# Half of d_ff as seven block products for eight, and w_in kept in DRAM: a packed-attention and FFN kernel on one core

## The chip, the cores and the metric

The kernel runs on one core of one Trainium2 chip. The metric is the device time of one execution in microseconds; several runs of one kernel are summed up by their median. The engines are named as the profile names them: PE (TensorE, matrix products; PEld are its weight loads), DVE (VectorE), ACT (ScalarE), POOL (GpSimd), SP (SyncE, which issues nearly all DMAs). Each takes its instructions from a queue of its own, in order, and waits on semaphores for the others.

## The reference

Two small attentions, one behind the other, feed a feed-forward product. There are 8 batches, 8 heads, 576 rows of 64 columns, and 32 packed rows p for each head. All data is float32.

```python
p_packed = sm_attn(p, k, v)             # softmax(p k^T / 8) v : 32 rows a head
attn_out = sm_attn(q, p_packed, p_packed)
x = attn_out.transpose(0, 2, 1, 3).reshape(B * S, H * D)   # 4608 x 512
h = x @ w_in                            # 512 x 2048
g = h * np.clip(h + 3.0, 0.0, 6.0) / 6.0
out = g @ w_out                         # 2048 x 512
```

## The kernel before

**Numbers.** Each float32 operand of the two large products is split into a high part that TensorE takes in one pass and a low part, the rest; a product is three matmuls: high by high, high by low, low by high. For x @ w_in the kernel does not form x: it multiplies w_in by the packed rows first (m, 256 by 2048 for a batch, `u_m`, matmuls at L339, split at L525 and L527), and the first product is then m by the attention weights a.

**Tiles.** d_ff is cut into 16 tiles f of 128, d_model stays whole, 512 columns, one PSUM bank. The 576 rows of a batch go through in two chunks, c = 0 and c = 1; one is narrow (256 rows) and one wide (320 rows: 256 and an edge of 64). The edges of an even batch and the odd one after it are joined to one block of 128 rows, which the wide chunk of the odd batch multiplies. In even batches the wide chunk is c = 1, in odd ones c = 0. A step s = 16c + f of batch b does:
- `first_product`: six matmuls (L921) into one of two PSUM tiles `ps_hh`, 256 or 320 columns each;
- `gated`: relu on ACT (L933), min and multiply on DVE (L934), the cast to the high part on ACT (L940), the low part on POOL (L941); edges alike (L946, L947);
- `second_product` (L952): three matmuls of 512 columns for each 128 rows, into accumulators that stay open over the 16 steps. Its call is put into `pend` and made two steps later, so that two first products lie between a gate and its use.

At f = 15 the accumulators are scaled on ACT (L911) and stored (L912).

**Order.** Batch 0 follows a list written by hand (`PLAN`). For batches 1 to 7 the Tile scheduler orders the instructions; `fill(c, f)` gives it, ahead of each step, pieces of the next batch's work: three chains (`inputs`: loads and transposes of k and q; `packed`: the first attention and its product with v; `ahead`: the second attention's weights `u_s2`), begun at the steps that `STAGES` names, so many pieces a step. From step `SOON` = 24 the first two quarters of the next batch's m are made, `u_m(b+1, 0, 1)`, as one block of 32 small matmuls on TensorE; the last two are made at the start of that batch, `u_m(b, 2, 3)`, spread by `LATE`. w_in stays in SBUF throughout as four tiles of 1 MB, one for each quarter of d_ff (`w_in0` to `w_in3`). The packed attention's product with v (L458) reads `v_nat` and `v_high`, loaded on SP.

## Time and profile before

| | |
|---|---|
| median of 3 runs | 720.01 us (719.67 to 720.78) |
| profiled execution | span 718.5 us; its own time is among those of the runs, which lie 1.2 to 2.3 us above the span |
| mean granted TensorE clock in it | 0.990 |
| PE busy | 699.5 us, 97% |
| ACT, DVE, POOL busy | 387.9, 345.9, 255.2 us |
| DMA | 55.97 MB, mean 78 GB/s |

One execution is profiled; its span is counted from the first to the last instruction on the core. In rows that name a line, an engine, an operation and tiles (out<-in), the numbers behind the bar are busy time and the mean duration of one in ns, then the idle time of the engine ahead of them and what ended it. In timeline rows the first number is the start in us from the begin of the span, the second the duration; "x2" stands for two instructions in one row.

### The profile page before, as it was taken

How to read it: one execution, taken by the hardware profiler on the slowest of the kernel's cores; microseconds unless marked ns; L12 is line 12 of the kernel's file. 1: busy time of each engine (PE TensorE's matmuls, PEld its weight loads, DVE VectorE, ACT ScalarE, POOL GpSimd, SP SyncE). 2: the span in 40 equal slices, each digit the busy share in tenths (PEclk: the TensorE clock that was granted, in tenths of full speed). 3: DMA queues.
4: the chain of work that ended last, by engine and by line, in shares of the span. 5: the costliest groups of instructions: out<-in, count | busy, mean ns of one | idle time of the engine just before them, and what ended most of it. 6: DMA issues, size and time to landing. Idle time of an engine off the chain costs nothing.

```text
span 718.5 us, 13932 instructions
## 1 busy us (share of the span) xinstructions
PE 699.5 (97%) x5168; PEld 572.7 (80%) x5168; DVE 345.9 (48%) x725; ACT 387.9 (54%) x916; POOL 255.2 (36%) x391
## 2 busy tenths in 40 slices
PE   6599999999999999999999999999999999999998
PEld 4477877788788878888788888888878887888886
DVE  2887788341844274441555338433184426431111
ACT  5799976444555356543555446544455535553343
POOL 1565641232223344323322234332322324433332
PEclk9699999999999999999999999999999999999999
DMA  9989853335015510433104440133401510000010
GB/s 287 307 210 232 226 138 94 49 63 119 1 26 100 103 35 1 96 63 75 45 1 96 75 92 1 34 67 71 106 2 28 93 39 31 1 31 0 1 45 30
DMA packets 191029, 55.97 MB, mean 78 GB/s; under 512 B 172528, under 2 KB 184304, under 8 KB 190960
## 3 DMA queue, kind: packets, MB, share of 16 engines
q1 hardware_dynamic: 190416, 54.88, 32.7%
q8 instruction: 40, 0.66, 0.4%
q10 hardware_dynamic: 544, 0.20, 0.1%
q14 instruction: 29, 0.24, 0.1%
HBM read 45.61 MB, written 9.44 MB: 77 GB/s over the span
## 4 chain that ended last, share of the span: by engine, by line
PE 89%; DVE 3%; DMA 2%; ACT 2%; SPq 2%; issue 1%; POOL 0%; DVEq 0%; ACTq 0%
PE acc L952 53%; PE ps_hh L921 23%; PE ps_h L595 3%; PE ps L339 3%; PE ps_x L339 2%; SPq L284 1%; PE ps L458 1%; DMA nat<-in_q_dram 1%; DMA v_high<-in_v_dram 1%; PE ps_t L666 1%; DVE tr L543 1%; PE ps L428 1%; DMA k_nat<-in_k_dram 1%; PE ps L263 1%; PE ps_w L708 0%
## 5 line engine op out<-in xcount | busy, mean ns | idle before, releaser
L952 PE MATMUL acc<-wo_hi,g 128*128 128x512 f32 x896 | 319.0, 397 | 0.0
L941 POOL TENSOR_TENSOR g<-t,g 128x256 fp32r<-128x256 f32 x224 | 166.3, 743 | 408.1 <-ACT g L940 396.4
L934 DVE SCALAR_TENSOR_TENSOR t<-t,ps_hh 128x320 f32<-128x320 f32 (+1 forms) x224 | 100.9, 450 | 243.6 <-ACT t L933 242.7
L952 PEld LDWEIGHTS acc<-wo_hi,g 128*128 128x128 f32 x896 | 168.3, 188 | 42.8 <-issue 5.3
L933 ACT ACTIVATE t<-ps_hh,three 128x320 f32<-128x320 f32 (+1 forms) x224 | 111.9, 500 | 165.7 <-PE ps_hh L921 160.9
L952 PE MATMUL acc<-wo_lo,g 128*128 128x512 f32 x448 | 176.9, 395 | 0.0
L940 ACT CAST g<-t 128x256 fp32r<-128x256 f32 x224 | 90.8, 405 | 93.7 <-DVE t L934 92.2
L921 PE MATMUL ps_hh<-a_hi,m_hi 128*128 128x320 f32 (+1 forms) x448 | 133.9, 299 | 0.0
L921 PE MATMUL ps_hh<-a_hi,m_lo 128*128 128x320 f32 (+1 forms) x448 | 132.7, 296 | 0.0
L921 PE MATMUL ps_hh<-a_lo,m_hi 128*128 128x320 f32 (+1 forms) x448 | 132.7, 296 | 0.0
L921 PEld LDWEIGHTS ps_hh<-a_hi,m_hi 128*128 128x128 f32 x448 | 84.4, 188 | 11.9 <-issue 1.4
L952 PEld LDWEIGHTS acc<-wo_lo,g 128*128 128x128 f32 x448 | 84.7, 189 | 11.1 <-issue 0.8
L921 PEld LDWEIGHTS ps_hh<-a_lo,m_hi 128*128 128x128 f32 x448 | 84.6, 189 | 8.5
L921 PEld LDWEIGHTS ps_hh<-a_hi,m_lo 128*128 128x128 f32 x448 | 84.7, 189 | 0.9 <-issue 0.9
L543 DVE STREAM_TRANSPOSE tr<-nat 128x576 f32<-128x576 f32 x56 | 42.7, 768 | 36.8 <-DMA nat<-in_k_dram 19.2
L947 POOL TENSOR_TENSOR bnd_lo<-t,bnd_hi 128x64 fp32r<-128x64 f32 x112 | 39.4, 352 | 0.0
L946 ACT CAST bnd_hi<-t 128x64 fp32r<-128x64 f32 x112 | 27.0, 241 | 0.0
L952 PE MATMUL acc<-wo_hi,gh 128*128 128x512 f32 x64 | 26.2, 410 | 0.0
L952 PE MATMUL acc<-wo_lo,bnd_hi 128*128 128x512 f32 x64 | 25.3, 395 | 0.0
L952 PE MATMUL acc<-wo_hi,bnd_hi 128*128 128x512 f32 x64 | 25.1, 393 | 0.0
L952 PE MATMUL acc<-wo_hi,gl 128*128 128x512 f32 x64 | 25.1, 393 | 0.0
L952 PE MATMUL acc<-wo_hi,bnd_lo 128*128 128x512 f32 x64 | 25.1, 392 | 0.0
(181 smaller groups left out, 838.0 us busy)
## 6 DMA issues: line engine op xcount, KB each, us to landing
out_dram<-osb SPq DMA_DIRECT2D x36, 256.0 KB, 2.2
nat<-in_k_dram SPq DMA_DIRECT2D x112, 72.0 KB, 2.6
nat<-in_q_dram SPq DMA_DIRECT2D x112, 72.0 KB, 2.5
raw_out<-in_moe_w_out_dram SPq DMA_DIRECT2D x10, 512.0 KB, 5.1
raw_in<-in_moe_w_in_dram SPq DMA_DIRECT2D x10, 512.0 KB, 5.3
v_nat<-in_v_dram SPq DMA_DIRECT2D x28, 128.0 KB, 2.7
v_high<-in_v_dram SPq DMA_DIRECT2D x56, 64.0 KB, 2.2
raw<-in_moe_w_out_dram SPq DMA_DIRECT2D x4, 512.0 KB, 6.9
```

Of the source, the lines that this page charges most:

```text
L263: nc.tensor.matmul(banks[x][NPK * a:NPK * a + NPK, :n * P], state["pp"][half, NPAIR * x + a], cols[half, :, a], start=True, stop=True,)
L339: nc.tensor.matmul(pair[x][NPK * a:NPK * a + NPK, :n], rows[half, a], c, start=True, stop=True)
L543: nc.vector.transpose(out=t, in_=state.pop(("nat", which, b, a)))
L595: nc.tensor.matmul(h[:, hf, :HS], mm[:, g, fs], aa[:, hf * HS:(hf + 1) * HS], start=(g == 0 and i == 0), stop=(g == NG - 1 and i == 2),)
L921: state["first"] = nc.tensor.matmul(h[:, :n], mm[:, g, fs], aa[:, t0:t0 + n], start=(g == 0 and i == 0), stop=(g == NG - 1 and i == 2),)
L933: state["relu"] = nc.scalar.activation(out=t[:, :n], in_=h, func=AF.Relu, bias=three)
L934: state["gate"] = nc.vector.scalar_tensor_tensor(out=t[:, :n], in0=t[:, :n], scalar=6.0, in1=h, op0=ALU.min, op1=ALU.mult)
L940: nc.scalar.copy(out=gh, in_=tm)
L941: nc.gpsimd.tensor_sub(out=gl, in0=tm, in1=gh.bitcast(F32))
L946: nc.scalar.copy(out=bh, in_=tb)
L947: nc.gpsimd.tensor_sub(out=bnd_lo[:, slot:slot + REM], in0=tb, in1=bh.bitcast(F32))
L952: nc.tensor.matmul(acc, gg, wo_at(part, f), start=(f == 0 and i == 0), stop=(f == NF - 1 and i == 2),)
```

## The change

**Pairs.** From batch 2 on, tiles f = 0 to 7 are taken as four pairs. For a pair (f, f+1) and 256 rows the second product is a 2x2 by 2x2 block product (row blocks of 128 by the two tiles; the two tiles by the two 256-column halves of w_out). It is done with Strassen's scheme in Winograd's form: seven block products instead of eight, each of three matmuls of 256 columns, on sums of blocks. Tiles 8 to 15 stay as they were ("singles").

- Sums of the gated tiles: four DVE instructions of 128 columns for a pair, behind the odd step's gate; then splits on ACT and POOL of 256, 512 and 128 columns (`split`).
- Sums of w_out: `T1`, `T2`, `T4` with their splits go into the buffers of w_in1 to w_in3, T3 over a half of w_out itself. They are made once, in the second chunk of batch 1 (`combine`, a third of a pair's yields a step from f = 4 on).
- Four accumulators A to D (`roles`): A and B take their block products and all singles; C and D are summed at the last pair (one ACT copy, one POOL add, three DVE instructions) and added to A and B at the end by DVE, where ACT copied before.
- The product of the joined edges takes a pair's tiles with the sums that are there, nine matmuls (three of 512 columns, six of 256) instead of six of 512. Edges are kept as float32 (`bnd`) and split late (`edge_parts`).

**w_in.** Since its buffers are taken, w_in is written to DRAM in batch 1 (`keep_w_in`, four DMAs of 1 MB), and for each later batch fetched back one quarter at a time into the one buffer left (`fetch_w_in`). `v_nat` takes turns in that buffer. So m is made in blocks of one quarter: 0, 1, 2 from step 21 on, quarter 3 in the first steps of the next batch. `u_s2` takes one half of the rows at a time in batches 3 to 7, and `STAGES` for the later batches lets the packed attention start at step 10 and takes one piece of the last chain a step.

```diff
-STAGES = ((0, 1), (6, 2), (19, 2))
-
-
-SOON = 24
-LATE = ((3, 2, 1, 2, 1), (3, 1, 1, 1, 0))
+STAGES = (((0, 1), (6, 2), (19, 2)), ((0, 1), (10, 2), (19, 1)))
+
+
+LATE = (3, 2, 1, 2, 1)
+PAIRS = 4
...
-        t = state["v", b] = ap.tile([P, NPAIR, NST, D], F32, name="v_nat", tag="v_nat", bufs=1)
+        home, tag = (wr, "w_in0") if steady else (wp, "v_nat")
+        t = state["v", b] = home.tile([P, NPAIR, NST, D], F32, name="v_nat", tag=tag, bufs=1)
...
+    def edge_product(acc, f, hi, lo, summed, first, last):
+
...
+        i = f // 2
+        second_product(f, acc, *lhs(0), first=first, last=False)
+        product(acc[:, :H2], lhs(1), block(i, "B21"))
+        product(acc[:, H2:], lhs(2), block(i, "B22"))
...
+    def combine(i):
+
...
+        x = [xp.tile([P, 6 * P], F32, name="wx", tag="raw") for _ in range(2)]
+        for k in range(2):
+            hi, lo = (wo_at(part, 2 * i + k).bitcast(F32) for part in ("hi", "lo"))
+            nc.gpsimd.tensor_tensor(out=x[k][:, :DM], in0=hi, in1=lo, op=ALU.add)
+            yield
+        b11, b12, t1 = (x[0][:, k * H2:(k + 1) * H2] for k in range(3))
+        b21, b22, t2 = (x[1][:, k * H2:(k + 1) * H2] for k in range(3))
+        nc.vector.tensor_sub(out=t1, in0=b12, in1=b11)
+        nc.vector.tensor_sub(out=t2, in0=b22, in1=t1)
+        yield
+        nc.vector.tensor_sub(out=b12, in0=b12, in1=b22)
+        nc.vector.tensor_sub(out=b21, in0=b21, in1=t2)
+        yield
+        for name, made in (("T1", t1), ("T2", t2), ("T4", b21), ("T3", b12)):
+            hi, lo = block(i, name)
+            nc.scalar.copy(out=hi, in_=made)
+            nc.vector.tensor_sub(out=lo, in0=made, in1=hi.bitcast(F32))
+            yield
+
+    def moe_pairs(b, c, fill):
+
+        even = b % 2 == 0
+        wide = (c == 1) == even
...
+        def pair_product(i, hi0, lo0, hi1, lo1):
+            at = {"A11": 0, "S1": 1, "S2": 2, "S3": 3, "A12": 4, "A22": 5, "S4": 6}
+
+            def lhs(name):
+                k = at[name]
+                return [(z[k // 4])[:, (k % 4) * P:(k % 4 + 1) * P] for z in ((hi0, hi1), (lo0, lo1))]
+
+            order = [
+                ("A", 0, "A12", "B21"), ("B", 0, "A22", "T4"), ("C", 0, "A11", "B11"), ("D", 0, "S1", "T1"),
+                ("C", 1, "S2", "T2"), ("D", 1, "S3", "T3"), ("A", 1, "S4", "B22"),
+            ]
+            if i == 0:
+                order = order[2:6] + order[:2] + order[6:]
+            for x, half, l, r in order:
+                fresh = x not in banks
+                product(
+                    bank(x)[:, half * H2:half * H2 + H2], lhs(l), block(i, r), fresh,
+                    i == PAIRS - 1 and x in "CD",
+                )
+            if i == PAIRS - 1:
+                sixth = 1.0 / 6.0
+                r1, r2 = (gp.tile([P, DM], F32, name="osb") for _ in range(2))
+                made["r"] = r1, r2
+                nc.scalar.activation(out=r1, in_=bank("C"), func=AF.Copy, scale=sixth)
+                u1 = r2[:, H2:]
+                nc.gpsimd.tensor_tensor(out=u1, in0=r1[:, :H2], in1=r1[:, H2:], op=ALU.add)
...
+                added(r1[:, H2:], 0, u1)
+                added(r2[:, :H2], 1, u1)
+                added(r2[:, H2:], 0, r2[:, :H2])
+
+        def single_product(f, gh, gl):
+            for k, x in enumerate("AB"):
+                second_product(f, bank(x), gh[:, k * P:(k + 1) * P], gl[:, k * P:(k + 1) * P], first=False)
+                if f == NF - 1:
+                    r = made["r"][k]
+                    nc.vector.scalar_tensor_tensor(
+                        out=r, in0=bank(x), scalar=1.0 / 6.0, in1=r, op0=ALU.mult, op1=ALU.add
+                    )
+                    nc.sync.dma_start(out=out[row + k * P:row + (k + 1) * P], in_=r)
...
+        for f in range(NF):
+            fill(f)
+            h = first_product(b, f, t0, n)
+            if f < 2 * PAIRS:
+                i = f // 2
+                if f % 2 == 0:
+                    ta = gp.tile([P, WT], F32, name="t")
+                    gate_into(ta, h, n)
...
+                    second(1)
+                    continue
+                tb = xp.tile([P, W + P], F32, name="tb", tag="tb")
+                gate_into(tb, h, n)
+                x = xp.tile([P, 6 * P], F32R, name="ga", tag="raw")
+                hi1, lo1 = x[:, :3 * P], x[:, 3 * P:]
+                split(hi1[:, :2 * P], lo1[:, :2 * P], tb[:, off:off + 2 * P])
...
+                a1, a2 = (ta[:, off + k * P:off + (k + 1) * P] for k in range(2))
+                b1, b2 = (tb[:, off + k * P:off + (k + 1) * P] for k in range(2))
+                s2, s3 = (ta[:, W + k * P:W + (k + 1) * P] for k in range(2))
+                s4 = tb[:, W:W + P]
+                nc.vector.tensor_sub(out=s3, in0=a2, in1=a1)
+                nc.vector.tensor_add(out=a2, in0=a2, in1=b2)
+                nc.vector.tensor_sub(out=s2, in0=a2, in1=a1)
+                state["gate"] = nc.vector.tensor_sub(out=s4, in0=b1, in1=s2)
+                hi0, lo0 = (gp.tile([P, 4 * P], F32R, name=f"g{y}", tag="g", bufs=4) for y in "hl")
+                if off:
+                    four = ta[:, off:off + 4 * P].rearrange("p (a n) -> p a n", a=2)
+                else:
+                    four = ta.rearrange("p (a n) -> p a n", a=2)[:, :, :2 * P]
+                split(*(y.rearrange("p (a n) -> p a n", a=2) for y in (hi0, lo0)), four)
+                split(hi1[:, 2 * P:], lo1[:, 2 * P:], s4)
+                pend.append(lambda i=i, parts=(hi0, lo0, hi1, lo1): pair_product(i, *parts))
+                second(1)
+                continue
...
+    xp = ctx.enter_context(tc.tile_pool(name="xp", bufs=2))
+    dram = ctx.enter_context(tc.tile_pool(name="dram", bufs=1, space=bass.MemoryType.DRAM))
+    w_kept = dram.tile([NCH, P, FPC * DM], F32, name="w_kept")
+
+    def keep_w_in(n):
+        nc.sync.dma_start(out=w_kept[n], in_=w_in_sb[n].rearrange("p f a e -> p (f a e)"))
+
+    def fetch_w_in(n):
+        t = w_in_sb[n] = wr.tile([P, FPC, NPAIR, P], F32, name="w_again", tag="w_in0")
+        nc.sync.dma_start(out=t.rearrange("p f a e -> p (f a e)"), in_=w_kept[n])
+
+    def first_quarters(b):
+
+        for n in range(NCH - 1):
+            fetch_w_in(n)
+            yield
+            yield
+            yield from coarse(u_m(b, n))
...
-                for _ in range(LATE[b > 1][s] if s < len(LATE[0]) else 0):
-                    next(late, None)
-                if s >= SOON:
+                if b == 1:
+                    for _ in range(LATE[s] if s < len(LATE) else 0):
+                        next(late, None)
+                    if s < NCH:
+                        keep_w_in(s)
+                    for i in range(PAIRS):
+                        if c and f >= 2 * i + 4:
+                            for _ in range(3):
+                                next(turned[i], None)
+                else:
+                    if s > 0:
+                        next(late, None)
+                if s >= 21:
                     next(soon, None)
+                if s == 31 and more:
+                    rest(soon)
+                    fetch_w_in(NCH - 1)
             with tc.issue_after(state["load"].ins), behind_gates():
-                for chain, (start, count) in zip((inputs, packed, ahead), STAGES):
+                for chain, (start, count) in zip((inputs, packed, ahead), STAGES[b > 1]):
                     for _ in range(count if s >= start else 0):
                         next(chain, None)
 
```

On TensorE, in batch 7, second chunk: L952 before, two d_ff tiles of which one is shown (`g_8173` is the tile of high and low parts; `wo_hi`, `wo_lo` the parts of w_out).

```order
L921 MATMUL ps_hh<-a_hi,m_lo 128x256
L952 MATMUL acc<-wo_hi,g_8173 128x512 [waits Activation_49]
L952 MATMUL acc<-wo_lo,g_8173 128x512
L952 MATMUL acc<-wo_hi,g_8173 128x512
L952 MATMUL acc<-wo_lo,g_8173 128x512
L952 MATMUL acc<-wo_hi,g_8173 128x512 [waits Pool_49]
L952 MATMUL acc<-wo_hi,g_8173 128x512
L921 MATMUL ps_hh<-a_hi,m_hi 128x256 [waits DVE_49]
```

The same place after the change; `ga` and `gh` hold high parts of the tiles and of their sums (`gl` the low ones), `wt_` the sums of w_out.

```order
L919 MATMUL ps_hh<-a_hi,m_lo 128x256
L952 MATMUL acc<-wo_hi,ga 128x256 [waits Activation_49]
L952 MATMUL acc<-wo_lo,ga 128x256
L952 MATMUL acc<-wt_2327,ga 128x256 x2
L952 MATMUL acc<-wo_hi,ga 128x256 [waits Pool_49]
L952 MATMUL acc<-wt_2327,ga 128x256
L952 MATMUL acc<-wo_hi,gh 128x256 [waits Activation_49]
L952 MATMUL acc<-wo_lo,gh 128x256
L952 MATMUL acc<-wt_2329,gh 128x256 x2
L952 MATMUL acc<-wo_hi,ga 128x256 [waits Activation_49]
L952 MATMUL acc<-wo_lo,ga 128x256
L919 MATMUL ps_hh<-a_hi,m_hi 128x256 [waits DVE_49]
```

One d_ff tile was six matmuls of 512 columns with a wait for ACT and one for POOL; now 12 of the 21 matmuls of a pair stand together, then a first product, then the other nine.

On TensorE, at the end of a batch, the product that makes m: before, two quarters from two tiles of w_in in one block, with nothing but buffers to wait for (the first of these rows is a first product).

```order
L921 MATMUL ps_hh<-a_hi,m_lo 128x320
L339 MATMUL ps_x<-w_in_sb_562,pps 32x512 [waits PE_49] x2
L339 MATMUL ps_x<-w_in_sb_562,pps 32x512 x6
L339 MATMUL ps_7409<-w_in_sb_326,pps 32x512 [waits PE_49]
L339 MATMUL ps_7409<-w_in_sb_326,pps 32x512 x7
L952 MATMUL acc<-wo_hi,g_7341 128x512 [waits Activation_49]
```

After, the third quarter of batch 7, from the tile that was fetched (`w_again`), with a wait for its DMA; the fourth comes 34 rows later, alike.

```order
L952 MATMUL acc<-wo_hi,g_8431 128x512
L952 MATMUL acc<-wo_lo,g_8431 128x512
L340 MATMUL ps_8465<-w_again,pps 32x512 [waits DMAHW2_49,DVE_49,PE_49]
L340 MATMUL ps_8465<-w_again,pps 32x512 x7
L952 MATMUL acc<-wo_hi,g_8431 128x512 [waits Pool_49]
L952 MATMUL acc<-wo_hi,g_8431 128x512
```

The block is halved, and stands alone between matmuls of a second product; the read of w_in now waits for a queue of DMA.

On SP, at the end of the first of these batches: the loads of the next k and the stores of the output before.

```order
L398 DMA v_nat<-in_v_dram 64x4x64 [waits DMAHW4_49]
L398 DMA v_nat<-in_v_dram 64x4x64 [waits DMAHW5_49]
L912 DMA out_dram<-osb 128x512 [waits DMAHW6_49,Activation_49]
L912 DMA out_dram<-osb 128x512 [waits DMAHW7_49,Activation_49]
L284 DMA nat<-in_k_dram 32x18x32 [waits DMAHW0_49,DVE_49]
L284 DMA nat<-in_k_dram 32x18x32 [waits DMAHW1_49]
L284 DMA nat<-in_k_dram 32x18x32 [waits DMAHW2_49]
```

And after, with the fetches of w_in among them.

```order
L284 DMA nat<-in_k_dram 32x18x32 [waits DMAHW2_49]
L1339 DMA w_again<-w_kept 128x2048 [waits DMAHW3_49,PE_49]
L1339 DMA w_again<-w_kept 128x2048 [waits DMAHW4_49,DMAHW3_49,PE_49]
L1339 DMA w_again<-w_kept 128x2048 [waits DMAHW5_49,DMAHW4_49,PE_49]
L284 DMA nat<-in_k_dram 32x18x32 [waits DMAHW6_49,DVE_49]
L284 DMA nat<-in_k_dram 32x18x32 [waits DMAHW7_49]
L284 DMA nat<-in_k_dram 32x18x32 [waits DMAHW0_49]
```

Three fetches, each of which waits for TensorE to have read the quarter before, now stand ahead of k loads and stores in the one queue of SP.

194 lines of the change are left out of this document (141 added, 53 removed).

## The prediction

> **What bounds the kernel now.** The page comes first: the busy shares, the chain that ended last, and the costliest groups.
>
> ```profile
> ## 1 busy us (share of the span) xinstructions
> PE 699.5 (97%) x5168; PEld 572.7 (80%) x5168; DVE 345.9 (48%) x725; ACT 387.9 (54%) x916; POOL 255.2 (36%) x391
> ## 4 chain that ended last, share of the span: by engine, by line
> PE 89%; DVE 3%; DMA 2%; ACT 2%; SPq 2%; issue 1%; POOL 0%; DVEq 0%; ACTq 0%
> ...
> L952 PE MATMUL acc<-wo_hi,g 128*128 128x512 f32 x896 | 319.0, 397 | 0.0
> L941 POOL TENSOR_TENSOR g<-t,g 128x256 fp32r<-128x256 f32 x224 | 166.3, 743 | 408.1 <-ACT g L940 396.4
> ...
> L952 PEld LDWEIGHTS acc<-wo_hi,g 128*128 128x128 f32 x896 | 168.3, 188 | 42.8 <-issue 5.3
> ```
>
> TensorE is busy 97% of the span, carries 89% of the chain, and the second product (L952) has no idle time before it. So from batch 1 on the time is the sum of what TensorE streams, and a change counts by the TensorE time that it takes away, adds, or leaves empty. Busy time of a matmul is no price, since matmuls overlap (397 ns each); the price is the distance from one start to the next. The timeline of TensorE near the end, where batch 7 runs with no attention beside it, gives it.
>
> ```profile
> 690.84 0.28 PE L921 MATMUL ps_hh<-a_hi,m_hi 128*128 128x256 f32 x1
> ...
> 691.55 0.40 PE L952 MATMUL acc<-wo_hi,g 128*128 128x512 f32 x1
> ...
> 692.94 0.28 PE L921 MATMUL ps_hh<-a_hi,m_hi 128*128 128x256 f32 x1
> ```
>
> Six 256-column matmuls start in 691.55 − 690.84 = 0.71 us, 0.1185 us each; six 512-column ones in 692.94 − 691.55 = 1.39 us, 0.232 us each. Half the width costs 51% of the time.
>
> **The change part by part.** The sums stand against 720.0 us, the median of the runs shown: the profiled execution has a span of 718.5 us, and some 1.5 us lie outside the span, which the change leaves alone.
>
> *The pairs.* Before, two d_ff tiles took 12 matmuls of 512 columns: 12 × 0.232 = 2.784 us. Now they take 21 of 256: 21 × 0.1185 = 2.489 us. That saves 0.295 us a pair; 6 batches × 2 chunks × 4 pairs are 48 pairs, so **−14.2 us**. No row shows 256-column matmuls with seven different operands and four output halves, so the unit is bounded: at 0.113 us (0.95 of the row) a pair saves 0.41 us (−19.7 in all), at 0.125 it saves 0.16 us (−7.6). I take the row's value.
>
> The matmuls double in number against their width, and each loads its own weights. The row of loads above says 188 ns for one load, yet full-array 256-column matmuls, each with a load of its own, start every 0.1185 us: loads lie beside matmuls. The Trainium skill, page "TensorE: Matmul & The Clock Gate", section "The mechanism", speaks against the change: by it a weight load overlaps a running matmul only when the two use different row groups, which 128×128 loads never do. This trace disagrees for these rows.
>
> *Products of w_in, one quarter at a time.* A double block of two quarters and a single block of one are both in the trace:
>
> ```profile
> 356.62 0.28 PE L921 MATMUL ps_hh<-a_hi,m_lo 128*128 128x256 f32 x1
> 356.82 1.09 PE L339 MATMUL ps_x<-w_in_sb,pps 64*32 64x512 f32 x16
> ...
> 359.04 0.40 PE L952 MATMUL acc<-wo_lo,g 128*128 128x512 f32 x1
> ```
>
> ```profile
> 120.33 0.31 PE L921 MATMUL ps_hh<-a_hi,m_lo 128*128 128x320 f32 x1
> 120.57 1.09 PE L339 MATMUL ps<-w_in_sb,pps 64*32 64x512 f32 x16
> ...
> 121.84 0.31 PE L921 MATMUL ps_hh<-a_lo,m_hi 128*128 128x320 f32 x1
> ```
>
> The double takes 2.42 us less the two normal steps in it (0.12 + 0.23), 2.07 us; the single 1.51 − 2 × 0.1465 (320 columns, from the starts of its neighbours) = 1.22 us. Batches 2 to 7 have 12 doubles, which become 24 singles: 12 × (2.44 − 2.07) = **+4.4 us**.
>
> *Scores of the second attention, one half at a time* (batches 3 to 7). Both halves together, and a half of the same shape from the first attention:
>
> ```profile
> 348.97 0.28 PE L921 MATMUL ps_hh<-a_hi,m_lo 128*128 128x256 f32 x1
> 349.18 0.72 PE L339 MATMUL ps_x<-tr,pps 64*32 64x288 f32 x16
> ...
> 350.65 0.40 PE L952 MATMUL acc<-wo_lo,g 128*128 128x512 f32 x1
> ```
>
> ```profile
> 302.62 0.31 PE L921 MATMUL ps_hh<-a_hi,m_lo 128*128 128x320 f32 x1
> 302.86 0.72 PE L339 MATMUL ps<-tr,p_tr 64*32 64x288 f32 x16
> ...
> 303.85 0.39 PE L952 MATMUL acc<-wo_lo,g 128*128 128x512 f32 x1
> ```
>
> 1.68 − 0.35 = 1.33 us for both, 1.23 − 0.38 = 0.85 for one: 5 × (2 × 0.85 − 1.33) = **+1.8 us**. The joined edges in pairs (9 matmuls, 3 of 512 and 6 of 256, for 6 of 512) come to 1.41 us for 1.39, **+0.2 us** over 12 pairs.
>
> *The two waits of TensorE that go.* From 185 us on TensorE waits for a DMA in one place only:
>
> ```profile
> PE ps L458 <- DMA v_high<-in_v_dram: 1.4, 4, 0.5
> ```
>
> The packed attention of batches 4 and 6 waits for its v. In the new order that attention starts at step 10 instead of 6 of a batch, so its loads have some 8 us more: **−1.4 us**. Ends: 0, if the later load of v_nat (which now shares its buffer with w_in) eats the room, and −2.8.
>
> *Batch 1, second chunk.* Here the weight combinations are added: per pair two POOL adds of 512 columns, four DVE subtractions and four low parts of 256, four ACT casts.
>
> ```profile
> 170.00:203.00 33.00, 33.00 (x231) 26.87 (x230) 19.28 (x38) 17.21 (x39) 9.72 (x13) 1.00 0.12 37
> ```
>
> ```profile
> L1027 DVE TENSOR_TENSOR gl<-t,gh x15: 677/685/1722, 39.7 to 112.8; 128x512 fp32r<-128x512 f32 x15
> ...
> L1027 POOL TENSOR_TENSOR gl<-t,gh x1: 1293/1293/1293, 72.1 to 72.1; 128x512 fp32r<-128x512 f32 x1
> ```
>
> In these 33 us (columns: PE, PEld, DVE, ACT, POOL busy) DVE works 19.3 us. It gains 32 instructions of at least half of 685 ns, 11 us: 30 of 33, nearly full, while the gates that TensorE waits for stand in the same queue. POOL gains 8 × 1.29 = 10 us. And DVE and POOL slow each other:
>
> ```profile
> L503 DVE TENSOR_TENSOR z<-z,den x14: 740/757/1294, 104.0 to 610.5; 128x576 f32<-128x576 f32 x14
> ```
>
> ```profile
> 267.95 1.29 DVE L503 TENSOR_TENSOR z<-z,den 128x576 f32<-128x576 f32 x1
> ```
>
> ```profile
> 267.63 1.00 POOL L941 TENSOR_TENSOR g<-t,g 128x256 fp32r<-128x256 f32 x1 [1.51 <-ACT g L940]
> ```
>
> L503 has a median of 757 ns, and 1294 where POOL runs beside it; L941 then takes 1.00 us for its mean of 0.74. L503 has both inputs in SBUF, as all DVE instructions have that the combinations add. The Trainium skill, page "GPSIMD Engine Reference", section "1. Specifications", says that the SBUF interfaces are shared with VectorE and that DVE instructions with two SBUF inputs contend for them; the trace agrees (0.54 us lost by one instruction). I take **+2.0 us** of empty TensorE, between 0 (the rest fits into the 33 us) and 6 (a third on top of the 11 + 7 us of two-input work of DVE and POOL).
>
> *Operands of a pair.* Between the odd step's first product and its block products now stand relu, gate, three DVE sums of 128 columns (the fourth beside the cast), an ACT cast of 512 columns, and for the low parts a POOL subtraction of 512.
>
> ```profile
> L933 ACT ACTIVATE t<-ps_hh,three 128x256 f32<-128x256 f32 x112 | 53.0, 473 | 77.0 <-PE ps_hh L921 73.9 <-POOL g L941 2.6 <-issue 0.2
> L934 DVE SCALAR_TENSOR_TENSOR t<-t,ps_hh 128x256 f32<-128x256 f32 x112 | 46.8, 418 | 113.8 <-ACT t L933 113.1
> ...
> L1025 ACT CAST gh<-t 128x512 fp32r<-128x512 f32 x16 | 9.9, 621 | 1.1 <-DVE t L1020 1.1
> ```
>
> A 128-column sum is bounded by a quarter of 685 ns (0.17) and half of 685 (0.34); nearest is a quarter plus a start, 0.23. High parts: 0.47 + 0.42 + 0.7 + 0.62 = 2.2 us, with four hand-overs 2.6. Low parts: + 1.29 and the contention of 0.3 above = 4.2 us. In the new order of TensorE, 12 block products of the pair before, a first product, its last 9 and another first product come between: 1.43 + 0.71 + 1.07 + 0.71 = 3.9 us until the first high part is used, and 2.1 more until the low ones. So both have over 1 us of room: nothing in most pairs. Where attention work of ACT or DVE (0.6 to 0.8 us an instruction) falls between two links, the room is gone: **+1.0 us** over 48 pairs, from 0 to 19 (0.4 us in every pair, rival A). Without the cover each pair would cost its 2.6 us.
>
> *w_in from DRAM.* A quarter, 1 MB, is fetched once the product of the quarter before has read the buffer.
>
> ```profile
> out_dram<-osb SPq DMA_DIRECT2D x36, 256.0 KB, 2.2
> ...
> raw_in<-in_moe_w_in_dram SPq DMA_DIRECT2D x10, 512.0 KB, 5.3
> ```
>
> No row has 1 MB. The 512 KB took 5.3 us at the start of the kernel, with many loads at once; ends are 4.4 us (2 × 2.2) and 10.6 (2 × 5.3). In steady state few loads run beside it (the window above has a DMA share of 0.12), so I take 5.5, nearer to the row of 256 KB. In the new order TensorE has 8 to 10 us of other work between the first three quarters, but only 5.4 to 6.3 between the third and the fourth. With the hand-over to SyncE the fourth is late by some 0.2 us, six times: **+1.2 us**, from 0 to 29 (rival D). The fetches wait on SyncE ahead of k loads and stores of the output, which are needed some steps later. The four writes of w_in in batch 1 have nobody waiting for them. The last chunk ends with a DVE instruction where ACT copied: nothing.
>
> Sum: −14.2 + 4.4 + 1.8 + 0.2 − 1.4 + 2.0 + 1.0 + 1.2 = −5.0, so 720.0 − 5.0 = **715.0 us**.
>
> **The rivals.**
>
> *A, operands come late (slower).* The place is the wait of the first block product for the ACT cast, and of the low ones for POOL. The chain has 3.9 us for the high and 6.0 us for the low parts; from 0.10 us late in each pair beyond what is summed (5.0 / 48) the gain is gone. For it: POOL's 743 ns double, the contention of 1.29 for 0.76 us, and attention work in the same queues. Against it: over 1 us of room, and POOL at 36%. At 0.4 us a pair the change loses 19 us more than I take: 733 us; at 0.2 us, 724.
>
> *B, narrow matmuls cost more than half.* At 0.125 us each the pairs save 7.6 us instead of 14.2: 715.0 + 6.6 = 721.6 us at most, 719 to 721 with the other terms a little better. For it: the seven products change halves of four banks all the time, which no row of before does. Against it: the 0.1185 us hold for three different operands in turn.
>
> *C, loads are not hidden.* Were the rule of the section named above to hold, each 256-column matmul would be spaced by its load, 188 ns: 21 × 0.188 = 3.95 us for 2.78, +56 us for 48 pairs in place of −14.2: about 785 us. The row of 0.1185 us speaks against it.
>
> *D, the fourth quarter is late.* At 10.6 us a fetch TensorE waits 4.8 us six times: 715.0 + 29 − 1.2 = 743 us; at 7 us, 6 × 1.5 = 9 us, 723. It decides from 6.3 us a fetch on (0.2 + 5.0 / 6 us late). For it: the 512 KB row. Against it: the DMA share of 0.12 in the window of 170 to 203 us.
>
> That the change does not do what it says is ruled out by the order of TensorE, which has 21 rows of 256 columns for 12 of 512.
>
> **How the numbers follow.** Forecast 0.62, A 0.16, B 0.12, C 0.02, D 0.08. The forecast's own range goes from 707.5 (pairs at −19.7 and the small losses at half) to 718.5 (two losses at their ends, 3 to 4 us). To hold 8 in 10 the range takes in B and the milder half of A and D: 707.5 to 724. A measurement of this kernel tells 0.2%, 1.4 us, from no change. Faster by more: 0.62 and 0.03 of B, 0.65. Within: most of B and the mildest of A and D, 0.14. Slower: the rest, 0.21.
>
> **What would show it right or wrong.** The timeline of a pair late in batch 7 should show 21 matmuls in about 2.49 us; 2.62 or more is B, 3.9 is C. In batches 2 to 7 the waits of TensorE on ACT g or POOL for L952 should sum to a few us; 10 and more is A. A wait of TensorE for w_again of over 1 us each is D. The waits for v_high should be gone, and the gates of batch 1's second chunk should be the only place where TensorE waits for DVE. If TensorE is 97% busy again and the time is not near 715, the price of one of the blocks was wrong.

## The result, and the profile after

| | before | after |
|---|---|---|
| median, same chip | 719.84 us (719.15 to 720.78, 4 runs) | 727.83 us (727.18 to 728.73, 4 runs) |
| profiled execution, span | 718.5 us | 727.0 us |

The changed kernel takes 1.0113 times as long (95% interval 1.0098 to 1.0128): slower by 1.1%, where 0.7% faster was forecast. The time lies above the whole range.

Rows of the page of the changed kernel: busy shares, the chain that ended last, one group, and DMA issues.

```profile
PE 696.1 (96%) x5636; PEld 584.1 (80%) x5636; DVE 466.7 (64%) x1021; ACT 404.1 (56%) x884; POOL 354.2 (49%) x503
...
PE 79%; DVE 9%; DMA 5%; ACT 2%; SPq 2%; issue 2%; POOL 1%; ACTq 0%; POOLq 0%; DVEq 0%
...
L952 PE MATMUL acc<-wo_hi,g 128*128 128x512 f32 x512 | 182.6, 399 | 2.9 <-POOL g L937 2.9
...
w_again<-w_kept SPq DMA_DIRECT2D x24, 1024.0 KB, 4.9
...
w_kept<-w_in_sb SPq DMA_DIRECT2D x4, 1024.0 KB, 6.9
```

TensorE still looks full, at 96%. But the chain has 10 points less of TensorE than before and 6 more of DVE and 3 more of DMA: the time is lost in stretches where TensorE is not what is waited for. Where those are is read from the first gate (the DVE instruction on `ps_hh`) of a stretch. The timeline of DVE before, at the start of batch 1, of its second chunk, and of batch 2:

```profile
120.94 0.49 DVE L934 SCALAR_TENSOR_TENSOR t<-t,ps_hh 128x320 f32<-128x320 f32 x1 [1.54 <-ACT t L933]
...
170.05 0.42 DVE L934 SCALAR_TENSOR_TENSOR t<-t,ps_hh 128x256 f32<-128x256 f32 x1 [2.28 <-ACT t L933]
...
210.72 0.42 DVE L934 SCALAR_TENSOR_TENSOR t<-t,ps_hh 128x256 f32<-128x256 f32 x1 [1.56 <-ACT t L933]
```

The same three after:

```profile
127.09 0.49 DVE L931 SCALAR_TENSOR_TENSOR t<-t,ps_hh 128x320 f32<-128x320 f32 x1 [1.54 <-ACT t L930]
...
176.15 0.42 DVE L931 SCALAR_TENSOR_TENSOR t<-t,ps_hh 128x256 f32<-128x256 f32 x1 [2.91 <-issue]
...
222.01 0.42 DVE L931 SCALAR_TENSOR_TENSOR t<-t,ps_hh 128x256 f32<-128x256 f32 x1
```

| stretch | before | after | difference |
|---|---|---|---|
| up to batch 1 | 120.94 | 127.09 | **+6.1** |
| batch 1, first chunk | 49.1 | 49.1 | 0 |
| batch 1, second chunk | 40.7 | 45.9 | **+5.2** |
| batch 2 to the end of the span | 507.8 | 505.0 | −2.8 |

The pairs work: from batch 2 on the kernel is faster. Two places ahead of them cost 11.3 us.

**Batch 0: the stores of w_in.** The code calls `keep_w_in` in batch 1, but all four stores go out before batch 1 begins, at 41.04, 52.59, 78.01 and 98.87 us. The timeline of SP after the change shows the first two among batch 0's loads:

```profile
41.04 0.39 SPq L1335 DMA_DIRECT2D w_kept<-w_in_sb  x1
42.75 7.57 SPq L284 DMA_DIRECT2D nat<-in_k_dram  x8
...
52.59 0.55 SPq L1335 DMA_DIRECT2D w_kept<-w_in_sb  x1
53.23 7.56 SPq L284 DMA_DIRECT2D nat<-in_q_dram  x4
```

The same loads before, in SP's timeline:

```profile
43.40 5.41 SPq L284 DMA_DIRECT2D nat<-in_k_dram  x8
...
52.51 3.17 SPq L284 DMA_DIRECT2D nat<-in_q_dram  x4
```

With a store in front, four loads of q take 7.56 us to issue, not 3.17. DVE then waits for that q (in brackets: idle time, and what ended it). The first row is from before, where the same transpose began with no wait, the second from after:

```profile
62.47 0.77 DVE L543 STREAM_TRANSPOSE tr<-nat 128x576 f32<-128x576 f32 x1
...
65.31 0.78 DVE L545 STREAM_TRANSPOSE tr<-nat 128x576 f32<-128x576 f32 x1 [3.12 <-DMA nat<-in_q_dram]
```

Waiting is not the whole loss. At 89.39 us TensorE has waited 2.13 us for a gate of batch 0, and from 90.75 to 94.16 us its granted clock is 0.50 (columns: length, busy PE, PEld, DVE, ACT, POOL, then clock and DMA):

```profile
90.75:94.16 3.41, 3.41 (x85) 2.79 (x84) 1.03 (x4) 2.61 (x5) 2.50 (x2) 0.50 0.97 293
```

The same run of matmuls in TensorE's timeline, from its first row to its last, before and then after:

```profile
84.81 0.29 PE L595 MATMUL ps_h<-a_hi,m_hi 128*128 128x288 f32 x1
...
88.14 0.40 PE L952 MATMUL acc<-wo_lo,gh 128*128 128x512 f32 x1
```

```profile
89.39 0.40 PE L597 MATMUL ps_h<-a_hi,m_hi 128*128 128x288 f32 x1 [2.13 <-DVE t L1223]
...
94.27 0.39 PE L952 MATMUL acc<-wo_lo,gh 128*128 128x512 f32 x1
```

It took 3.33 us with the clock at 1.00, and takes 4.88 now: some 1.5 of the 6.1 us are a lower clock. At its end TensorE is 6.13 us late, and the loss is complete. SP's own waits up to 121 us have a new line as well, a store that waits for POOL to make w_in's quarter:

```profile
SPq L1335 <- POOL w_in_sb L197: 4.2, 1, 4.2
```

That is the fourth store, which waits from 94.6 to 98.8 us. It comes after the loss and adds nothing to it.

Nothing reads `w_kept` before batch 2, and nothing makes the stores wait for batch 1. The scheduler puts them where w_in is ready.

**Batch 1, second chunk: the combinations.** TensorE's waits from 115 to 230 us (total, times, longest):

```profile
PE acc L952 <- POOL g L937: 2.9, 3, 1.6
PE ps_hh L919 <- DVE t L931: 1.1, 3, 0.6
```

The chunk by windows (columns as above):

```profile
176.00:211.00 35.00, 32.58 (x218) 24.05 (x216) 28.10 (x56) 18.32 (x45) 17.19 (x17) 1.00 0.24 82
211.00:222.00 11.00, 9.21 (x61) 6.83 (x61) 8.79 (x18) 6.64 (x17) 6.89 (x7) 1.00 0.16 49
```

TensorE is idle for 2.4 and 1.8 us of these. DVE is at 80% of both windows, and its instructions are stretched: the four subtractions at L1059 differ by 3.7 times (min/median/max in ns).

```profile
L1059 DVE TENSOR_TENSOR wx<-wx x4: 412/760/1510, 184.2 to 213.2; 128x256 f32<-128x256 f32 x4
```

The longest, in DVE's timeline, and what POOL does beside it:

```profile
213.21 1.51 DVE L1059 TENSOR_TENSOR wx<-wx 128x256 f32<-128x256 f32 x1 [0.48 <-POOL wx L1055]
```

```profile
211.85 2.58 POOL L1055 TENSOR_TENSOR wx<-wo_hi,wo_lo 128x512 f32<-128x512 f32 x2 [2.73 <-DVE wt L1068]
214.40 1.82 POOL L937 TENSOR_TENSOR g<-t,g 128x256 fp32r<-128x256 f32 x2
```

The low part of a gated tile (L937) stands behind two 1.29 us adds for the combinations, and TensorE waits for it:

```profile
215.36 0.97 PE L952 MATMUL acc<-wo_hi,g 128*128 128x512 f32 x3 [1.60 <-POOL g L937]
```

**Batches 2 to 7.** A piece of a pair in batch 7, TensorE's timeline:

```profile
692.82 0.28 PE L919 MATMUL ps_hh<-a_hi,m_hi 128*128 128x256 f32 x1
...
693.18 0.28 PE L952 MATMUL acc<-wo_hi,ga 128*128 128x256 f32 x1
...
694.62 0.28 PE L952 MATMUL acc<-wo_hi,gl 128*128 128x256 f32 x1
```

Twelve block products start in 1.44 us, 0.120 each, and the three first products ahead of them in 0.36 us, 0.120 each too. All of TensorE's waits in this stretch (from 222 us on):

```profile
PE ps L340 <- DMA w_again<-w_kept: 1.2, 1, 1.2
PE acc L952 <- POOL gl L937: 1.0, 2, 0.5
PE ps_hh L919 <- DVE t L931: 0.6, 3, 0.2
```

No wait for `v_high` is left. Late operands are rare and short: by the distances between starts five come late, 2.5 us in all, 0.05 us a pair, and one fetch is late by 1.3 us. The two longer ones wait for a low part of 512 columns on POOL, and POOL had itself stood idle before it:

```profile
363.94 1.40 POOL L937 TENSOR_TENSOR gl<-t,gh 128x512 fp32r<-128x512 f32 x1 [3.31 <-DMA out_dram<-osb_j]
```

In the code `gl` and the output of the joined edges, `osb_j`, take turns in the same four buffers, so this low part waits until an output store has left its buffer.

### The profile page after: what moved, and what is told of

It reads as the page before. It is cut to its first block, busy times and chain, and to the rows that moved or that the text cites. A ratio compares the mean times of both kernels' runs of the same rounds, so it can differ in the third digit from the quotient of the medians.

```text
span 727.0 us, 15138 instructions
## 1 busy us (share of the span) xinstructions
PE 696.1 (96%) x5636; PEld 584.1 (80%) x5636; DVE 466.7 (64%) x1021; ACT 404.1 (56%) x884; POOL 354.2 (49%) x503
## 4 chain that ended last, share of the span: by engine, by line
PE 79%; DVE 9%; DMA 5%; ACT 2%; SPq 2%; issue 2%; POOL 1%; ACTq 0%; POOLq 0%; DVEq 0%
PE acc L952 46%; PE ps_hh L919 23%; PE ps L340 5%; PE ps_h L597 2%; PE ps L460 1%; DMA room<-in_q_dram 1%; DMA w_again<-w_kept 1%; DVE t L931 1%; DMA out_dram<-osb_j 1%; PE ps L430 1%; SPq L284 1%; DMA raw_out<-in_moe_w_out_dram 1%; DMA raw_in<-in_moe_w_in_dram 1%; DVE z L505 1%; DMA p_nat<-in_p_dram 1%
## 5 line engine op out<-in xcount | busy, mean ns | idle before, releaser
L952 PE MATMUL acc<-wo_hi,g 128*128 128x512 f32 x512 | 182.6, 399 | 2.9 <-POOL g L937 2.9
L937 POOL TENSOR_TENSOR g<-t,g 128x256 fp32r<-128x256 f32 x128 | 101.5, 794 | 86.2 <-ACT g L936 69.2
L952 PEld LDWEIGHTS acc<-wo_hi,g 128*128 128x128 f32 x512 | 94.8, 188 | 30.4 <-POOL g L937 6.5
L952 PE MATMUL acc<-wo_lo,g 128*128 128x512 f32 x256 | 100.9, 394 | 0.0
L937 POOL TENSOR_TENSOR ga<-tb,ga 128x256 fp32r<-128x256 f32 x96 | 59.9, 625 | 57.8 <-ACT ga L936 52.0
L937 POOL TENSOR_TENSOR gl<-t,gh 128x512 fp32r<-128x512 f32 x48 | 64.1, 1335 | 18.6 <-DMA out_dram<-osb_j 6.3
L952 PE MATMUL acc<-wo_hi,gl 128*128 128x256 f32 (+1 forms) x160 | 52.5, 328 | 2.3 <-DVE gl L1230 1.3
L952 PE MATMUL acc<-wo_hi,gh 128*128 128x256 f32 (+1 forms) x160 | 54.0, 337 | 0.0
L952 PEld LDWEIGHTS acc<-wo_lo,g 128*128 128x128 f32 x256 | 48.3, 189 | 6.9 <-issue 0.8
L952 PE MATMUL acc<-wo_hi,ga 128*128 128x256 f32 x192 | 53.1, 283 | 0.0
L952 PE MATMUL acc<-wo_lo,gh 128*128 128x256 f32 (+1 forms) x160 | 52.1, 326 | 0.0
```

The lines of the kernel that those rows point to most:

```text
L937: nc.gpsimd.tensor_sub(out=lo, in0=x, in1=hi.bitcast(F32))
L952: nc.tensor.matmul(out, lhs[x], rhs[y], start=first and i == 0, stop=last and i == 2, skip_group_check=True)
```

## The experiments

Each kernel ran beside the kernel before, on one chip; ratios are to that kernel, with 95% intervals.

### The stores: later, and alone

The stores are held behind a load that ends late in batch 0:

```diff
                     if s < NCH:
-                        keep_w_in(s)
+                        with tc.issue_after(state["load"].ins):
+                            keep_w_in(s)
```

> The changed kernel, with the four writes of w_in to DRAM bound behind the last weight load on SP. Theory S (the writes, which the scheduler put between the weight loads of batch 0, cost the 6.1 us by which batch 1 begins later): its first gate is back at 121 us (127.1 in the changed kernel, 120.9 before), the time falls by 5.5 to 6.5 us to 721.5 to 722.3. Rival L (the new places of tiles, or the edges kept raw, slow batch 0): the first gate stays at 126 to 127, the time at 727 to 728.

Measured: 724.32 us (722.2 to 729.42, 10 runs), ratio 1.0070 (1.0047 to 1.0094). The first store now goes out at 97 us, and in the profiled run batch 1 begins at 122.2 us, against 127.09 after the change and 120.94 before. The second chunk of batch 1 stays at 45.8 us. The profiled run is the fastest of the ten; their median lies above the 721.5 to 722.3 us that were expected, and the other three stores go out from 106.5 to 107.5 us, still in batch 0.

And the stores put into the kernel before, with nothing else of the change:

```diff
+    w_kept = dram.tile([NCH, P, FPC * DM], F32, name="w_kept")
+    def keep_w_in(n):
+        nc.sync.dma_start(out=w_kept[n], in_=w_in_sb[n].rearrange("p f a e -> p (f a e)"))
...
                     next(late, None)
+                if b == 1 and s < NCH:
+                    keep_w_in(s)
```

> The kernel before with nothing added but the four writes of w_in to DRAM, which nobody reads; on SP they stand in the same rows as in the changed kernel. Theory S: the first gate of batch 1 moves from 120.9 to about 127 us and the time rises by 5 to 6.5 us to 725 to 726. Rival L: no change, 719.5 to 720.5.

Measured: 728.50 us (725.96 to 729.01, 4 runs), ratio 1.0105 (1.0082 to 1.0129). DVE's timeline has the first gate 9.3 us later than before, and each later chunk has the length that it has before:

```profile
130.24 0.49 DVE L934 SCALAR_TENSOR_TENSOR t<-t,ps_hh 128x320 f32<-128x320 f32 x1 [1.55 <-ACT t L933]
```

So four DMAs for which nobody waits cost as much as the whole loss, by themselves: they were taken out of batch 1 and put ahead of loads. It is more than was expected (725 to 726 us), and the price is not the same in every execution: 6.1 us in the change, 9.3 here (8.2 by the medians), and 4.4 and 4.5 in the next two kernels, which have the same stores in batch 0 and begin batch 1 at 125.31 and 125.46 us. The clock is a part of the difference: it is 0.50 for 3.41 us here as after the change, from 93.6 us on, and stays at 1.00 at this place in the other two. SP's wait for POOL is not: it ends at 102 us, when TensorE is already 9.2 us late. How the rest divides between SP's queue and the 4 MB themselves was not separated.

### The combinations left out

A block of w_out stands in for each sum of w_out, with the pairs as they are, so the output is another:

```diff
-        if name in ("T1", "T2", "T4"):
-            return blocks[i, name]
+        name = {"T1": "B11", "T2": "B21", "T3": "B12", "T4": "B22"}.get(name, name)
...
-            turned = [combine(i) for i in range(PAIRS)]
+            turned = []
```

> The changed kernel without the combinations of w_out: the block products read blocks of w_out in their places, so the output is another, and every matmul stays in place. Theory C (DVE and POOL, which the combinations load in the second chunk of batch 1 and which slow each other, make the gates late): that chunk falls from 45.9 to 40 to 41 us and the time by 5 to 6 us, to 722 to 723. Rival F (the single products of w_in and their fetched quarters make that chunk longer): it stays at 44 to 46 us, the time at 726.5 to 728.

Measured: 725.36 us (720.92 to 730.19, 10 runs), ratio 1.0067 (1.0040 to 1.0094). The second chunk of batch 1 takes 40.1 us (45.9 with the combinations), and TensorE waits nowhere in it: they cost 5.8 us. Not all of it shows in the time, which was expected at 722 to 723 us. Batch 2 begins earlier, and the fetch of its fourth quarter becomes late; beside this wait the clock is 0.50 for 3.41 us, from 220.3 us on. The two largest of TensorE's waits from 160 us on:

```profile
PE ps L340 <- DMA w_again<-w_kept: 2.6, 1, 2.6
PE ps L340 <- DVE tb L1173: 1.3, 1, 1.3
```

### The pairs left out

All else stays, with w_in kept and fetched; the second product is made of singles, and there are no combinations.

```diff
-PAIRS = 4
+PAIRS = 0
...
-                banks[x] = acc_of(roles["ABCD".index(x)])
+                banks[x] = next_acc()
...
+                    store(bank(x), out[row + k * P:row + (k + 1) * P])
```

> The changed kernel with all 16 tiles as singles, without combinations; w_in is still written and fetched, its product made by single quarters, the second attention by halves from batch 3 on, edges raw. Priced from the trace of the changed kernel: without the pairs' 12.5 us, without 5.5 us of batch 1 and without 1 to 2.6 us of late operands: 732 to 735 us. If the pairs pay nothing (rival: their gain is lost in waits that the records do not show), 722 to 727.

Measured: 732.05 us (729.48 to 733.43, 4 runs), ratio 1.0168 (1.0147 to 1.0189). From batch 2's first gate to the last gate of the kernel it takes 505.4 us, against 497.6 with pairs (222.01 to 719.57) and 500.6 before. The pairs are worth 7.9 us net. Of that, 21 × 0.120 = 2.52 us for the 2.784 of before give 0.264 × 48 = 12.7 us, and late operands and fetches of the paired kernel take back 3.8; some 1 us is not accounted for. These are two single executions, and this one is the fastest of its four, 2.6 us below their median; by the medians, with the 5.8 us of the combinations, the pairs come to some 10 us (732.05 − 727.83 + 5.8).

### The blocks made smaller, alone

In the kernel before, the products of w_in by single quarters and the scores by halves, without pairs or DRAM:

```diff
-        for part in both_halves(True, pps[b % 2], qt):
+        for part in both_halves(b <= 2, pps[b % 2], qt):
...
-        late = coarse(part for n in range(1, NCH) for part in u_m(1, n)) if b == 1 else coarse(u_m(b, 2, 3))
-        soon = coarse(u_m(b + 1, 0, 1)) if more else iter(())
+        late = coarse(part for n in range(1, NCH) for part in u_m(1, n)) if b == 1 else coarse(part for n in (2, 3) for part in u_m(b, n))
+        soon = coarse(part for n in (0, 1) for part in u_m(b + 1, n)) if more else iter(())
```

> The kernel before, with w_in in SBUF as before, but the product of w_in by single quarters in batches 2 to 7 and the second attention's scores by halves from batch 3 on. By the blocks of the trace: 12 x 0.37 + 5 x 0.37 = 6.3 us more, 726 to 727 us. Rival (TensorE has slack that takes the smaller blocks): under 2 us more, 720 to 722.

Measured: 724.76 us (724.39 to 725.03, 4 runs), ratio 1.0067 (1.0050 to 1.0084): 4.8 us, where 6.3 were expected and the rival had under 2. The forecast had 4.4 + 1.8 − 1.4 = 4.8 for these blocks and the end of the waits for v. Here those waits fall from 1.4 us to this, in TensorE's waits:

```profile
PE ps L458 <- DMA v_high<-in_v_dram: 0.5, 2, 0.3
```

The order of the attention is not changed here, and stores_alone, whose batches 2 to 7 are those of before, has 0.5 us of them too. So these waits differ from one execution to the next, and without their fall the smaller blocks cost some 5.7 us, for 6.2 in the forecast.

### The stores behind the last work of batch 0

From here on the question is whether both losses can be taken away. First the stores behind the last output of batch 0:

```diff
-            nc.sync.dma_start(out=rows, in_=osb)
+            state["stored"] = nc.sync.dma_start(out=rows, in_=osb)
...
-                        keep_w_in(s)
+                        with tc.issue_after(state["stored"].ins):
+                            keep_w_in(s)
```

> The changed kernel with the four writes of w_in bound behind the last store of batch 0, so that no byte of them moves while batch 0 loads its weights. Theory S: the first gate of batch 1 is at 120.5 to 121.5 us in every run, the time is 721 to 722.5 us and scatters less than stores_later did (722 to 729). Rival (writes between loads are not all of it; batch 0 is slower by the raw edges or the new places of tiles): the gate stays at 122 or later.

Measured: 722.05 us (720.98 to 723.07, 5 runs), ratio 1.0034 (1.0020 to 1.0048). Batch 1 begins at 121.77 us, 5.3 earlier than after the change, and the second chunk of batch 1 still takes 46.6 us. Of the two losses this leaves that of the combinations; the time is 2.3 us above the kernel before.

### The combinations spread over batch 1

On top of that, pairs 0 and 1 are combined in the first chunk (a buffer of w_in free by then holds the sums), pairs 2 and 3 in the second:

```diff
-            turned = [combine(i) for i in range(PAIRS)]
+            turned = chain(combine(0), combine(1))
+            turned_last = chain(*(combine_last(i) for i in range(2)), *(f(i) for i in (2, 3) for f in (combine, combine_last)))
...
+                    for _ in range(3 if s >= 10 else 0):
+                        next(turned, None)
+                    if c and f >= 4:
+                        if f == 4:
+                            rest(turned)
+                        for _ in range(2):
+                            next(turned_last, None)
```

T3 of pair 1 is written over its half of w_out before the last product of batch 1 with that half, so a part of batch 1's output is another; every instruction is there.

> As stores_after_batch0, and the combinations of w_out for pairs 0 and 1 are made in the first chunk of batch 1 (with scratch in the buffer of w_in1), those of pairs 2 and 3 over steps 5 to 12 of the second. Theory C (what counts is how many two-input instructions of DVE and POOL meet the gates): the second chunk falls from 45.9 to 41 to 43 us, the time to 717 to 719.5. Rival (the same DVE work costs the same wherever it is): the first chunk gets longer by what the second loses, 721 to 722.5.

Measured: 722.56 us (722.48 to 723.75, 4 runs), ratio 1.0042 (1.0027 to 1.0057): no gain over the run above. The first chunk took the combinations of two pairs for nothing (49.0 us), but the second still takes 45.6. The largest wait of TensorE in it, and DVE's timeline just ahead of it:

```profile
196.55 0.39 PE L920 MATMUL ps_hh<-a_hi,m_hi 128*128 128x256 f32 x1 [2.87 <-DVE t L932]
```

```profile
193.39 1.51 DVE L1076 TENSOR_TENSOR wo_lo<-wx,wo_hi 128x256 fp32r<-128x256 f32 x1
194.83 0.68 DVE L530 TENSOR_TENSOR m_lo<-ps,m_hi 128x512 fp32r<-128x512 f32 x1
195.43 0.76 DVE L509 STREAM_TRANSPOSE at<-z 128x576 f32<-128x576 f32 x1
196.12 0.37 DVE L932 SCALAR_TENSOR_TENSOR t<-t,ps_hh 128x256 f32<-128x256 f32 x1
```

The gate (L932) stands behind a combination stretched to 1.51 us, a low part of m, and a transpose of the next batch's attention. About 1 us behind this wait the granted clock is 0.50 for 3.41 us:

```profile
197.50:200.90 3.40, 3.40 (x19) 2.77 (x26) 3.40 (x7) 1.58 (x5) 1.80 (x2) 0.50 0.00 0
```

So this run speaks for the place of the work and not its amount: the steps up to f = 8 are full of attention work, and from 203 us on DVE has time (5.7 us busy in the 12 that follow). Whether that is so is tried below.

### Spread, with the scores in both halves again

One more edit on that kernel, to win back the 1.8 us of the halves by a later start of the last chain:

```diff
-STAGES = (((0, 1), (6, 2), (19, 2)), ((0, 1), (10, 2), (19, 1)))
+STAGES = (((0, 1), (6, 2), (19, 2)), ((0, 1), (10, 2), (24, 2)))
...
-        for part in both_halves(not roles, pps[b % 2], qt):
+        for part in both_halves(True, pps[b % 2], qt):
```

> As combine_spread, and the second attention's scores are taken with both halves at once again, from step 24 on, when banks C and D are free. By the blocks in the trace (0.84 us twice for 1.33) the time falls by 1.8 us more, to 715.5 to 717.7. Rival: the later start of that chain (step 24 for 19) makes the first products of the next batch late, and the time stays or rises.

Measured: 732.44 us (731.51 to 734.98, 4 runs), ratio 1.0181 (1.0157 to 1.0204), 1.4% above the kernel it starts from, where 715.5 to 717.7 us were expected. The two largest of TensorE's waits from 115 us on show what came in place of the 1.8 us:

```profile
PE ps L341 <- DMA w_again<-w_kept: 5.2, 5, 2.0
PE ps_hh L920 <- DVE t L932: 4.6, 3, 2.9
```

The fetches are late five times, where combine_spread has one such wait of 1.7 us. The longest of the second row, 2.9 us, stands in batch 1 and is in combine_spread too.

### The combinations at the end of the second chunk

As combine_spread, but pairs 2 and 3 begin at f = 9:

```diff
-                    if c and f >= 4:
-                        if f == 4:
+                    if c and f >= 5:
+                        if f == 5:
                             rest(turned)
-                        for _ in range(2):
+                        for _ in range(1 if f < 7 else 2 if f >= 9 else 0):
                             next(turned_last, None)
```

> As stores_after_batch0, with the combinations of pairs 0 and 1 in the first chunk of batch 1 (their T3 at steps 5 and 6 of the second) and those of pairs 2 and 3 from step 9 of the second on, where the trace of combine_spread shows DVE with free time (203 to 214 us). Theory C (the gates are late where the combinations and the attention's DVE work stand together): the second chunk falls from 46 to 41 to 43 us, the time to 717.5 to 719.5. Rival (any place of these instructions on DVE and POOL costs the same 5 us): it stays at 45 to 47 us, 721.5 to 723.

Measured: **715.97 us** (714.31 to 722.04, 12 runs), ratio 0.9952 (0.9933 to 0.9970): faster than the changed kernel and than the kernel before. The second chunk of batch 1 in DVE's timeline, from its first gate to that of batch 2:

```profile
170.21 0.42 DVE L932 SCALAR_TENSOR_TENSOR t<-t,ps_hh 128x256 f32<-128x256 f32 x1 [0.39 <-issue]
...
210.33 0.42 DVE L932 SCALAR_TENSOR_TENSOR t<-t,ps_hh 128x256 f32<-128x256 f32 x1 [0.21 <-ACT t L931]
```

That is 40.1 us, as without any combinations, and less than the 41 to 43 expected; the time too is below the 717.5 to 719.5 us that were expected. TensorE is busy throughout both windows of it, with DVE at 67% and then 85%:

```profile
170.00:203.00 33.00, 33.00 (x231) 26.24 (x230) 22.25 (x48) 18.50 (x44) 13.28 (x15) 1.00 0.48 141
203.00:211.00 8.00, 8.00 (x56) 6.00 (x55) 6.83 (x16) 4.97 (x13) 3.79 (x5) 1.00 0.18 57
```

### The fourth quarter's product later

On the same kernel, the product that waits for the last fetch begins four steps later:

```diff
-                    if s > 0:
+                    if s > 4:
                         next(late, None)
```

> As combine_tail, and the product of the last quarter of w_in is made from step 5 of a batch on instead of step 1, which gives its fetch 8 to 9 us beside other work of TensorE instead of 5.4 to 6.3. If late fetches are the waits for w_again that single executions show (0 to 2.6 us), they are gone from the trace and the time falls by 0.5 to 2 us against combine_tail: 716.5 to 718.5. Rival: the fetch that comes later makes v_nat late, which has the same buffer, and the waits move to L460 for v: no gain.

Measured: 716.72 us (713.96 to 718.94, 6 runs), ratio 0.9938 (0.9917 to 0.9959). TensorE waits for no fetch any more, but the intervals of this kernel and the one above overlap: they can't be told apart. In its profiled run, the slowest of the six, batch 1 begins at 124.5 us, 3.2 later than in combine_tail's, though no store stands in batch 0 in either. The two traces show where this arises: SP issues the same loads in the same order, and they land later here from the first on, a piece of w_out by 0.3 us at 8.9 us, another by 3.0 at 49.6, a third by 4.5 at 68.6. Why the transfers take longer was not found.

## Why the prediction was wrong

**The stores: the step that failed.** The prediction says: "The four writes of w_in in batch 1 have nobody waiting for them." The second half is true, and for that reason the first is not: with no reader until batch 2 and no order to keep them, the stores went into batch 0, and what waited was everything behind them on SP. The term was 0; it is 6.1 us in the change, 9.3 alone, and with the stores behind batch 0 the kernel gains 5.8 us (727.83 to 722.05). Some 1.5 of the 6.1 us are TensorE's clock at 0.50 behind one of the waits, a cost that no term of the prediction has. The prediction looked at SP at the fetches, and not at where the stores stood; SP's order of instructions, which is fixed before any run, has them among batch 0's loads.

**The combinations: right place, wrong size.** +2.0 us were taken, within 0 to 6; no_combine has 5.8 (45.9 for 40.1). The prediction saw DVE nearly full and the contention with POOL, and then took that most of it would fit. The Trainium skill, page "GPSIMD Engine Reference", section "1. Specifications", on which it leaned, says that DVE instructions with two inputs in SBUF contend with POOL. The trace agrees: such an instruction took from 0.41 to 1.51 us, the longest beside a POOL add. But combine_tail, where batch 1 with the same instructions is no longer than without them, shows that the price is not the work, it is its place in the two queues.

**The pairs: 12.7 of 14.2 us.** The unit of 0.1185 us was read off six starts in steps of 10 ns; over twelve it is 0.120, for block products and first products alike. Rival B, block products dearer than other matmuls of their width, did not happen, nor did C: 188 ns loads lie beside matmuls that start every 0.120 us.

**Smaller blocks, halves and v: 4.8 us, as forecast**, measured alone, and in part by luck: the blocks cost 5.7 us for 6.2, and the waits for v fell by 0.9 for 1.4, without the later start that was to end them. The joined edges were not tried by themselves.

**Operands and fetches: 3.8 us for 2.2.** Rival A did not come about: 0.05 us a pair, where it needed 0.10. The longest of these waits are not of the kind that was described, work in the same queues: there POOL waited for a buffer that an output store still held. Rival D appears once in a run: 1 MB landed in 4.9 us in the median (forecast 5.5), the six fetches of a fourth quarter in 4.8 to 6.6, where it was to decide from 6.3 on. The slowest of the six was 1.3 us late, and one in no_combine 2.6.

Together: −12.7 + 4.8 + 0.2 + 3.8 + 5.8 + 6.1 = +8.0 us, where the medians differ by 8.0; that it fits so well is luck, since some 1 us of the pairs is not accounted for and the 6.1 is that of one execution. Without the last two, −3.9 is left; combine_tail, which takes both away, gains 4.3 by the medians (715.97 for 720.25), 3.5 by the ratio. So most of the gain that was forecast is real, and it was lost in two places of batches 0 and 1, ahead of the first pair.

## What to carry to other kernels

An instruction that nobody waits for can still delay those behind it, so look up where the scheduler puts it in its queue, and tie it to work that has ended if it must not be early. Work done once, on engines that look free on average, belongs in the steps where their queues are free: the same combinations cost 5.8 us in one place, and nothing with half of them a chunk earlier and half at the chunk's end. An algebraic saving is to be judged with its preparation: here 12.7 us saved in the products were outweighed by what had to be made, stored and cut smaller for them.

## What the runs showed of the hardware

- A DVE subtraction of 128x256 with both inputs in SBUF took from 412 to 1510 ns (L1059), the longest beside a POOL add with two inputs in SBUF.
- With a 1 MB store ahead of them, four DMA issues of q took 7.56 us on SP's queue for 3.17.
- A fetch of 1 MB landed in 4.9 us (median of 24), less than the 5.8 of a 512 KB load in the crowded start of the same execution.
- The granted TensorE clock is 0.50 for 3.41 us, once each, in five of the profiled executions between 40 us and the end of the span (after the change, stores_alone, no_combine, combine_spread, spread_and_halves), each time beside a wait of TensorE of 2.0 to 3.3 us. Two waits as long, 3.27 us in no_combine at 89 us and 2.85 in spread_and_halves at 197 us, have none beside them, and from 40 us on no wait of 1.98 us or less has.
- The length of batch 0 differs by up to 3.9 us between profiled runs whose batch 0 holds no store (first gate at 120.55 us in combine_spread, 124.46 in later_quarter). Between combine_tail and later_quarter it is the loads that land later, in the same order; why stays open.
